# Twenty small additions from VectorE to POOL, squares behind halves, three moved instructions: a top-k attention with two feed-forward layers on one core

## The chip, the cores and the metric

One core of a Trainium2 chip runs the whole program as one launch. The metric is device microseconds (us) of that core, the median of several executions. Engines are named as the profile does: PE is TensorE's matmul, PEld its weight load, DVE is VectorE, ACT is ScalarE, POOL is GpSimd, SP is SyncE, which issues the DMAs.

## What is computed

The inputs are q, k and v (4 batches, 8 heads, 576 rows, 64 columns each), two weight matrices and a gain vector for the first feed-forward layer and two weight matrices for the second, all float32.

```python
scores = scale * np.matmul(q, k.transpose(0, 1, 3, 2))
kth = np.partition(scores, -top_k, axis=-1)[..., -top_k:-top_k + 1]   # top_k = 32
scores = np.where(scores >= kth, scores, -1000000000.0)
attn = np.exp(scores - np.max(scores, axis=-1, keepdims=True))
attn = attn / (np.sum(attn, axis=-1, keepdims=True) + 1e-09)
x = np.matmul(attn, v)                       # then rows (4*576, 8*64)
h = x @ w_in
e = np.exp(h - h_max)
solu = h * e / (np.sum(e, axis=-1, keepdims=True) + 1e-09)
x2 = ((solu - mu) / np.sqrt(var + 1e-06) * g_ln) @ w_out
h2 = x2 @ w_in2
out = (h2 * (1.0 / (1.0 + np.exp(-1.702 * h2)))) @ w_out2
```

## The kernel before, in words

`layers` is written twice into the program. The first copy (`quick`) works with constant scales and, beside its results, gathers sums by which it judges at its end whether those scales were fit: `insq` and `qsq` (sums of squares of the inputs), `zsq`, `ysum`. From them it makes a flag; all engines load the flag (L58) and branch (L59), and the second, exact copy runs only if the flag is set. It does not run for these inputs.

Every float32 operand of a matmul is held as two float16 halves: `split` (L120) makes a high half `hi` on ACT and a low half `raw - hi` on POOL or DVE. Where a total is wanted, a `Square` activation with an accumulator stands ahead of the halves and writes its junk into the tile of the high half. For k and q the two halves go into the tile `kq`, of which there is one (tag `kq`; the first few use other tags), and from there by a transposing DMA into `kt` (L359) or `qt` (L411).

Attention goes in 72 steps (two heads of 128 rows each): `scores` on PE, `copy_s` on ACT, `fold` (L473 to L476) and four `rounds` (L484, L487) on DVE that find the 32nd largest score, `mask` and `exp_of` on ACT and POOL, `high`/`low`, a transposing DMA, and three steps later `back`, the product with v. When a block's last step is through `back`, `finish` takes the reciprocals of the row sums (`recip`, L626 to L629), scales the result (L644) and queues the block for the feed-forward layers. These run interleaved with the attention steps, some blocks late; the last blocks run alone at the end. In the first six steps the 48 weight tiles are decoded and split on DVE, ACT and POOL (L249 to L254, L291, L138).

`recip` is the one place in the steps where DVE reads two operands that both lie in SBUF:

```python
def recip(r, n):
    nc.vector.scalar_tensor_tensor(r[:, 0:n], r[:, 0:n], 1e-9, r[:, 0:n], op0=ALU.add, op1=ALU.max)
    nc.vector.reciprocal(r, r)
```

It runs 20 times: 16 full blocks (8 sums a row) and 4 half blocks (4 sums).

Each engine runs its instructions in one fixed order. That order isn't the source's: the building layer places the instructions of each copy by its own estimate of when each can start, so a small edit can move instructions far away from it. The text below names the first copy alone.

Of the kernel before, what the change touches and what calls it, by code (L numbers as in the profile page):

```python
# [80 lines left out]
def layers(ctx, tc, quick, q, k, v, w1, w2, g_ln, w3, w4, out):  # L81
# [24 lines left out]
    if quick:  # L106
        picks = cst.tile([128, B * S * H // 128, 3], F32, name="picks")
        pickc = cst.tile([128, 2, 3], F32, name="pickc")
        insq = cst.tile([128, 2 * B * NP + 24], F32, name="insq")
        qsq = cst.tile([128, B * (NEWT + 1)], F32, name="qsq")  # L110
        zsq = cst.tile([128, NBLK], F32, name="zsq")
        ysum = cst.tile([128, NBLK], F32, name="ysum")
        for i, x in enumerate((1.0, -S_EXP, BIG)):
            nc.vector.memset(pickc[:, :, i], x)
        ones = cst.tile([128, 128], F32, name="ones")
        nc.gpsimd.memset(ones, 1.0)
# [3 lines left out]
    def split(raw, hi, lo, scale, what, total=None):  # L120

        n = lo_n[what] = lo_n.get(what, -1) + 1
        how = LO[what][n % len(LO[what])]
        if how == "P" and scale is not None:
# [3 lines left out]
        if how == "A" and scale is not None:  # L128
            act(raw, raw, AF.Copy, scale=scale)
            if total is not None:  # L130
                act(hi, raw, AF.Square, scale=1.0 / scale, accum_out=total)
            scale = None
        elif total is not None:
            act(hi, raw, AF.Square, accum_out=total)
        if scale is None:
# [3 lines left out]
        else:  # L139
            act(hi, raw, AF.Copy, scale=scale)  # L140
            nc.vector.scalar_tensor_tensor(lo, raw, scale, hi, op0=ALU.mult, op1=ALU.subtract)
        return how

# [44 lines left out]
    mhalf = cst.tile([128, 1], F32, name="mhalf")  # L188
    nc.vector.memset(mhalf, -0.5)
    wraw = {}  # L190

# [434 lines left out]
    def recip(r, n):  # L626

        nc.vector.scalar_tensor_tensor(r[:, 0:n], r[:, 0:n], 1e-9, r[:, 0:n], op0=ALU.add, op1=ALU.max)
        nc.vector.reciprocal(r, r)  # L629
# [66 lines left out]
    class Block:  # L696
# [121 lines left out]
        def g_high(self, g):  # L818
            t, gh = self.gh[g]
            if not quick:  # L820
                act(t, t, AF.Copy, scale=2.0 ** -16)
            act(gh[:, 0], t.rearrange("p (a n) -> p a n", a=4))

# [12 lines left out]
        def store(self):  # L836
            y = at.tile([128, 512], F32, tag="t", name="y")
            if quick:
                act(y, self.o, AF.Copy, scale=0.5 / (S_X2 * S_W[2] * S_W[3]), accum_out=ysum[:, self.no:self.no + 1])
            else:  # L840
                act(y, self.o, AF.Copy, scale=self.cf[:, 1:2])
# [65 lines left out]

    nc.sync.dma_start(gl, g_ln.rearrange("(c p) -> p c", p=128))
    if quick:
        nc.vector.tensor_scalar(gl, gl, S_W[1], None, op0=ALU.mult)  # L910

    if not quick:
        for a, b in ((0, 8), (8, 16), (16, WCH)):
            for i in range(a, min(a + RING, b)):
# [98 lines left out]
    gate = last_t[0]  # L1013
    load_for(0)
    with tc.issue_after(gate.ins):
# [14 lines left out]
    t = 0  # L1030
# [74 lines left out]

    ok = sm.tile([128, 6], F32, tag="ok", name="ok")

# [23 lines left out]
    nc.vector.tensor_scalar(flag, rows, 0.5, None, op0=ALU.is_gt)  # L1131
    return flag[0:1, 0:1]
# [30 lines left out]
```

## Time and profile before

| what | value |
|---|---|
| median of 3 runs | 961.12 us (960.68 to 962.55) |
| the profiled execution | 967.89 us, its span 966.0 us |
| busy: PE, DVE, ACT, POOL | 766.2, 766.7, 722.9, 695.9 us |
| mean granted TensorE clock | 0.914 of full speed |

The span is the time from the first to the last instruction; 1.9 us lie around it. Busy time is an average over stages: DVE is busy nearly without a break up to about 215 us, PE nearly without a break from about 300 us on, and after about 845 us the attention is over and PE runs the last feed-forward blocks.

### The profile page before, as it was taken

The page shows a single profiled execution, that of the slowest core. Times are in us where ns is not written, and L with a number is a line of the kernel's source. Part 1 is how long each engine was busy: PE and PEld are TensorE (multiplying, and loading weights), DVE is VectorE, ACT ScalarE, POOL GpSimd, SP SyncE. Part 2 cuts the span into 40 slices and gives each one's busy share as a digit, 9 for nine tenths or more (in the row PEclk, how much of TensorE's full clock was granted, in tenths as well). Part 3 has the DMA queues.
Part 4 walks back from the last instruction along what each step waited for, and adds up shares of the span by engine and source line. Part 5 has one row for each costly group of instructions (what it writes and reads, how often), then busy time and mean ns, then how long its engine had stood idle before and what let it go on. Part 6 is the DMA issues. An engine that isn't in the chain of part 4 may idle for free.

```text
span 966.0 us, 22236 instructions
## 1 busy us (share of the span) xinstructions
PE 766.2 (79%) x8228; PEld 497.6 (52%) x8228; DVE 766.7 (79%) x2150; ACT 722.9 (75%) x1257; POOL 695.9 (72%) x699
## 2 busy tenths in 40 slices
PE   1122524566688899989999899898999899999996
PEld 0011211534355556656665666565665666666564
DVE  4999999988698999897889988887988899511221
ACT  4689898587888978778899877778997878834431
POOL 2488999778968788777899886777987777733311
PEclk9995756677899999999999999998999899999998
DMA  6998666556757767566778577568756745532200
GB/s 159 314 308 202 178 164 151 122 117 126 143 122 139 122 119 136 105 119 124 137 138 156 115 127 118 100 111 150 137 113 116 130 76 90 97 69 45 44 14 25
DMA packets 337733, 122.66 MB, mean 127 GB/s; under 512 B 315344, under 2 KB 329168, under 8 KB 337616
## 3 DMA queue, kind: packets, MB, share of 16 engines
q1 hardware_dynamic: 337616, 121.16, 61.7%
q8 instruction: 66, 1.08, 0.5%
q14 instruction: 51, 0.42, 0.1%
HBM read 39.85 MB, written 4.72 MB: 46 GB/s over the span
## 4 chain that ended last, share of the span: by engine, by line
PE 26%; ACT 16%; DVE 16%; DMA 15%; POOL 14%; issue 8%; SPq 4%; ACTq 0%; POOLq 0%; DVEq 0%
PE h L806 9%; PE o L833 7%; ACT s L160 4%; PE x L776 4%; DVE wk L484 4%; POOL eh L523 4%; DVE wk L487 4%; PE ha L709 3%; POOL s L505 3%; POOL wt L138 2%; PE sc L455 2%; DMA kt<-kq 2%; ACT kq L160 2%; DMA qt<-kq 2%; DMA et<-eh 2%
## 5 line engine op out<-in xcount | busy, mean ns | idle before, releaser
L484 DVE MAX8 wk<-wk 128x8 f32<-128x296 f32 x576 | 242.2, 461 | 0.0
L806 PE MATMUL h<-x2t,wt 128*128 128x128 f16 x3456 | 217.1, 225 | 20.1 <-DVE t L815 14.8
L806 PEld LDWEIGHTS <-wt 128*128 128x128 f16 x3456 | 206.8, 101 | 27.2 <-issue 15.7
L833 PE MATMUL o<-wt,gh 128*128 128x512 f16 x864 | 203.3, 385 | 9.7 <-DVE wt L254 7.6
L523 POOL TENSOR_TENSOR eh<-s,eh 128x576 f16<-128x576 f32 x144 | 181.5, 1283 | 38.8 <-ACT eh L160 26.2
L505 POOL TENSOR_TENSOR s<-s,r 128x576 f32<-128x576 f32 x144 | 181.8, 1283 | 34.7 <-ACT r L160 34.5
L487 DVE MATCH_REPLACE8 wk<-wk 128x296 f32<-128x296 f32 x432 | 193.6, 458 | 0.0
L455 PE MATMUL sc<-kt,qt 128*128 128x64 f16 (+7 forms) x640 | 99.3, 321 | 71.7 <-DMA qt<-kq 30.8
L606 PE MATMUL av<-vt,et 128*128 128x64 f16 (+1 forms) x2400 | 90.1, 201 | 60.7 <-DMA et<-eh 52.2
L833 PEld LDWEIGHTS <-gh 128*128 128x128 f16 x864 | 83.8, 99 | 105.0 <-issue 16.1
L826 POOL TENSOR_TENSOR gh<-t,gh 128x512 f16<-128x512 f32 x72 | 83.6, 1161 | 73.2 <-ACT gh L160 73.1
L160 ACT ACTIVATE s<-s,picks 128x576 f32<-128x576 f32 x144 | 110.4, 768 | 16.9 <-POOL s L505 16.5
L606 PEld LDWEIGHTS <-et 128*128 128x128 f16 (+1 forms) x2400 | 82.2, 106 | 72.9 <-DMA et<-eh 55.9
L776 PE MATMUL x<-wt,zt 128*128 128x512 f16 x432 | 105.4, 397 | 14.3 <-DMA zt<-zh 14.2
L709 PE MATMUL ha<-wt,xt 128*128 128x512 f16 x432 | 101.9, 394 | 14.5 <-DMA xt<-xhl 11.1
L455 PEld LDWEIGHTS <-qt 128*128 128x128 f16 (+1 forms) x640 | 49.5, 110 | 123.5 <-DMA qt<-kq 31.2
L815 DVE SCALAR_TENSOR_TENSOR t<-t,h 128x512 f32<-128x512 f32 x72 | 49.2, 683 | 76.3 <-ACT t L160 73.3
L160 ACT ACTIVATE r<-s,picks 128x576 bf16<-128x576 f32 x144 | 103.5, 766 | 5.5 <-POOL picks L497 5.4
L160 ACT ACTIVATE t<-h 128x512 f32<-128x512 f32 x72 | 42.3, 588 | 70.7 <-PE h L806 61.9
L160 ACT ACTIVATE s<-sc 128x1152 f32<-128x1152 f32 x72 | 80.7, 1120 | 14.5 <-PE sc L455 8.5
L160 ACT ACTIVATE wt<-wt 128x512 f16<-128x512 f32 (+1 forms) x115 | 68.0, 627 | 22.9 <-DVE wt L254 10.5
L160 ACT ACTIVATE eh<-s 128x1152 f16<-128x1152 f32 x72 | 83.3, 1156 | 0.7
(84 smaller groups left out, 1070.1 us busy)
## 6 DMA issues: line engine op xcount, KB each, us to landing
wt<-in_moe_w_in_dram SPq DMA_DIRECT2D x24, 512.0 KB, 4.8
wt<-in_moe_w_out_dram SPq DMA_DIRECT2D x24, 512.0 KB, 5.7
qt<-qt SPq DMA_DIRECT2D x72, 64.0 KB, 2.0
raw<-in_k_dram SPq DMA_DIRECT2D x32, 128.0 KB, 2.5
raw<-in_q_dram SPq DMA_DIRECT2D x16, 256.0 KB, 3.3
vraw<-in_v_dram SPq DMA_DIRECT2D x32, 128.0 KB, 2.4
out_dram<-y SPq DMA_DIRECT2D x16, 256.0 KB, 3.2
et<-eh SPq DMA_TRANSPOSE x72, 4.7
```

The source lines that it names most:

```text
L160: nc.scalar.activation(out, in_, func, **kw)
L455: nc.tensor.matmul(sc[rows, i * S + c0:i * S + c1], t[qi // 4][:, hl, qi % 4, rows], kts[kp][:, k0 + c0:k0 + c1], start=(hl == 0), stop=(h ...
L484: nc.vector.max(out=wk[:, i, at_:at_ + 8], in_=wk[:, i, 0:W_END])
L487: nc.vector.match_replace(out=wk[:, i, 0:W_END], in_to_replace=wk[:, i, at_:at_ + 8], in_values=wk[:, i, 0:W_END], imm_value=LOW)
L505: nc.gpsimd.tensor_tensor(s[:, i], s[:, i], r[i], op=ALU.subtract)
L523: nc.gpsimd.tensor_tensor(eh[:, 1, cols], s[:, i], eh[:, 0, cols], op=ALU.subtract)
L606: nc.tensor.matmul(o[rows, col:col + 64], et[:, ea, 4 * i + c, rows], vts[kp][:, va, vc:vc + 64], start=(n == 0), stop=(n == 14))
L709: nc.tensor.matmul(h[:, half * 512:half * 512 + 512], self.xt[:, a, kc], w1v(kc, w, half), start=(n == 0), stop=(n == 11))
L776: nc.tensor.matmul(self.x2, self.zt[:, a, kc], w2v(kc, w), start=(n == 0), stop=(n == 23))
L806: nc.tensor.matmul(h2[:, mm * 128:(mm + 1) * 128], w3v(kc, w, 4 * g + mm), self.x2t[:, a, kc], start=(n == 0), stop=(n == 11))
L826: nc.gpsimd.tensor_tensor(gh[:, 1], t.rearrange("p (a n) -> p a n", a=4), gh[:, 0], op=ALU.subtract)
L833: nc.tensor.matmul(self.o, gh[:, a, mm], w4v(4 * g + mm, w), start=(g == 0 and n == 0), stop=(g == 3 and n == 11))
```

## The change

Five edits:

1. `recip`: the addition of 1e-9 (and a maximum that no longer is needed) leaves DVE and becomes a `tensor_scalar` on POOL. DVE's reciprocal now waits for POOL.
2. `split`: the `Square` for the totals comes behind the halves, and writes into a tile of its own, `squares`.
3. A one-column `Square` of a constant is put at the start of ACT's work, so that the one table load stands ahead of it.
4. The load of `g_ln` and its scaling go from the head of the program to behind the first k and q.
5. The last block's `ysum` is no longer judged. In its place the four gelu tiles of the last block are: their sums by the accumulator of the activation that makes the high half, their maxima by four new reductions on DVE. The final comparison loses one instruction.

```diff
     def split(raw, hi, lo, scale, what, total=None):
...
         if how == "A" and scale is not None:
             act(raw, raw, AF.Copy, scale=scale)
-            if total is not None:
-                act(hi, raw, AF.Square, scale=1.0 / scale, accum_out=total)
+            back = 1.0 / scale if total is not None else 1.0
             scale = None
-        elif total is not None:
-            act(hi, raw, AF.Square, accum_out=total)
...
+        if total is not None:
...
+            act(junk, raw, AF.Square, scale=back, accum_out=total)
...
+    if quick:
+        act(squares[:, 0:1], mhalf, AF.Square)
...
     def recip(r, n):
 
-        nc.vector.scalar_tensor_tensor(r[:, 0:n], r[:, 0:n], 1e-9, r[:, 0:n], op0=ALU.add, op1=ALU.max)
+        nc.gpsimd.tensor_scalar(r[:, 0:n], r[:, 0:n], 1.0, 1e-9, op0=ALU.mult, op1=ALU.add)
         nc.vector.reciprocal(r, r)
...
-            act(gh[:, 0], t.rearrange("p (a n) -> p a n", a=4))
+            if quick and self.no == NBLK - 1:
+                act(gh[:, 0], t.rearrange("p (a n) -> p a n", a=4), accum_out=glast[:, 0, g:g + 1])
+                nc.vector.tensor_reduce(glast[:, 1, g:g + 1], t, axis=AX.X, op=ALU.max)
...
     gate = last_t[0]
+    load_gl()
     load_for(0)
...
-    nc.vector.tensor_reduce(ok[:, 5:6], ok[:, 0:5], axis=AX.X, op=ALU.min)
-    bad = sm.tile([128, 1], F32, tag="bad", name="bad")
-    nc.vector.tensor_scalar(bad, ok[:, 5:6], 0.5, None, op0=ALU.is_lt)
+    nc.vector.tensor_scalar(ok[:, 5:9], glast[:, 0], 1e30, None, op0=ALU.is_le)
+    nc.vector.scalar_tensor_tensor(ok[:, 5:9], glast[:, 1], 65000.0, ok[:, 5:9], op0=ALU.is_le, op1=ALU.mult)
+    nc.vector.tensor_reduce(ok[:, 9:10], ok[:, 0:9], axis=AX.X, op=ALU.min)
...
-    nc.tensor.matmul(rows, ones, bad, start=True, stop=True)
+    nc.tensor.matmul(rows, ones, ok[:, 9:10], start=True, stop=True)
```

Lines of the changed kernel are some 5 to 16 higher. What the order of instructions becomes at three places:

ACT at the start of the program, before:

```order
L160 ACT_TABLE_LOAD
L160 ACTIVATE kq,insq<-raw 128x10x64
L160 ACTIVATE kq<-raw 128x10x64
L160 ACTIVATE kq,qsq<-raw 128x8x64
L160 ACTIVATE kq<-raw 128x8x64
L160 ACTIVATE wt<-wt 128x512 x3
```

and now:

```order
L164 ACT_TABLE_LOAD
L164 ACTIVATE squares<-mhalf 128x1
L164 ACTIVATE kq<-raw 128x10x64
L164 ACTIVATE squares,insq<-raw 128x640
L164 ACTIVATE kq<-raw 128x8x64
L164 ACTIVATE squares,qsq<-raw 128x512
L164 ACTIVATE wt<-wt 128x512 x6
```

The table load no longer stands behind a wait for k, and each high half is one activation nearer.

The third `recip` (in the weight decoding), on DVE before:

```order
L476 MAX wk<-sc 128x8 x2
L628 SCALAR_TENSOR_TENSOR rsum<-rsum 128x8
L253 SCALAR_TENSOR_TENSOR wi<-wt,wi 128x512
L484 MAX wk<-wk 128x8 x2
L629 RECIPROCAL rsum<-rsum 128x8
L254 SCALAR_TENSOR_TENSOR wt<-wt,wi 128x512
L487 MATCH_REPLACE wk<-wk 128x296 x2
```

now on DVE:

```order
L482 MAX wk<-sc 128x8 x2
L260 SCALAR_TENSOR_TENSOR wt<-wt,wi 128x512
L490 MAX wk<-wk 128x8 x2
L493 MATCH_REPLACE wk<-wk 128x296 x2
L490 MAX wk<-wk 128x8 x2
L493 MATCH_REPLACE wk<-wk 128x296
L635 RECIPROCAL rsum<-rsum 128x8
L493 MATCH_REPLACE wk<-wk 128x296
```

and the addition on POOL (L138 with `wt` is a low half, L297 a product of the decoding, L511 the mask, L529 the low half of the exponentials):

```order
L138 TENSOR_TENSOR wt<-wt 128x512 x2
L297 TENSOR_TENSOR wt<-wt 128x512
L634 TENSOR_SCALAR rsum<-rsum 128x8
L511 TENSOR_TENSOR s<-s,r 128x576 x2
L529 TENSOR_TENSOR eh<-s,eh 128x576 x2
```

The reciprocal moved behind the first rounds of the step, and the addition stands on POOL behind three large instructions of the decoding. The fifteenth addition stands on POOL directly behind the low half of a k tile (L138 with `kq`), and its reciprocal on DVE directly behind L798 (L792 before).

DVE at the end of the program, before:

```order
L815 SCALAR_TENSOR_TENSOR t<-t,h_13346 128x512
L1110 TENSOR_SCALAR junkc<-ysum 128x18
L1111 SCALAR_TENSOR_TENSOR junkc<-ysum,junkc 128x18
L1113 TENSOR_REDUCE ok<-junkc 128x1
L1125 TENSOR_REDUCE ok<-ok 128x1
L1127 TENSOR_SCALAR bad<-ok 128x1
L1131 TENSOR_SCALAR flag<-rows 128x1
```

and now:

```order
L821 SCALAR_TENSOR_TENSOR t<-t,h_13352 128x512
L830 TENSOR_REDUCE glast<-t 128x1
L1140 TENSOR_SCALAR ok<-glast 128x4
L1141 SCALAR_TENSOR_TENSOR ok<-glast,ok 128x4
L1142 TENSOR_REDUCE ok<-ok 128x1
L1146 TENSOR_SCALAR flag<-rows 128x1
```

The comparison of `ysum` went ahead of the last two gelu tiles, and nothing behind the last gelu waits for the last store's activation. On PE the small matmul of the flag (L1129 before, L1144 now) was the last one; now it stands ahead of the last four matmuls of the output.

## Rows read from the trace of the kernel before

**Rows 1.** Busy time by stretch: stretch, us, PE, PEld, DVE, ACT, POOL; clock, DMA, GB/s.

```profile
20.00:60.00 40.00, 6.89 (x26) 2.81 (x27) 39.47 (x101) 27.07 (x49) 21.52 (x24) 1.00 0.93 284
100.00:140.00 40.00, 15.01 (x164) 7.41 (x162) 38.25 (x97) 35.34 (x62) 37.93 (x37) 0.67 0.65 163
400.00:500.00 100.00, 92.08 (x1046) 60.46 (x1044) 84.74 (x248) 82.42 (x145) 81.03 (x86) 0.98 0.69 128
900.00:957.00 57.00, 54.09 (x535) 36.09 (x533) 12.88 (x29) 19.72 (x37) 13.44 (x13) 1.00 0.10 24
```

**Rows 2.** The page's part 4: the chain that ended last, shares by engine and line.

```profile
PE h L806 9%; PE o L833 7%; ACT s L160 4%; PE x L776 4%; DVE wk L484 4%; POOL eh L523 4%; DVE wk L487 4%; PE ha L709 3%; POOL s L505 3%; POOL wt L138 2%; PE sc L455 2%; DMA kt<-kq 2%; ACT kq L160 2%; DMA qt<-kq 2%; DMA et<-eh 2%
```

**Rows 3.** The same chain in order of time, the first 14 us: start, us, what.

```profile
0.73 0.46 SPq L908
...
5.30 1.28 ACT L160
...
6.60 0.84 ACT kq L160 x2
...
7.46 1.36 ACT kq L160 x3
...
10.71 2.72 DMA qt<-kq
```

**Rows 4.** Timeline, the load of q; and its group in the page's part 6.

```profile
3.79 0.60 SPq L389 DMA_DIRECT2D raw<-in_q_dram  x1
...
raw<-in_q_dram SPq DMA_DIRECT2D x16, 256.0 KB, 3.3
```

**Rows 5.** L628: ns, least, median, most; and its groups: busy us, mean ns | idle before.

```profile
L628 DVE SCALAR_TENSOR_TENSOR rsum<-rsum x20: 148/162/8205, 87.2 to 841.1; 128x8 f32<-128x8 f32 x16, 128x4 f32<-128x4 f32 x4
...
L628 DVE SCALAR_TENSOR_TENSOR rsum<-rsum 128x8 f32<-128x8 f32 x16 | 11.8, 736 | 1.9 <-ACT s L160 1.8
...
L628 DVE SCALAR_TENSOR_TENSOR rsum<-rsum 128x4 f32<-128x4 f32 x4 | 2.1, 534 | 1.0 <-ACT s L160 1.0
```

**Rows 6.** Timeline around the longest of them, DVE and POOL: start, us, [idle before <- releaser].

```profile
169.37 8.21 DVE L628 SCALAR_TENSOR_TENSOR rsum<-rsum 128x8 f32<-128x8 f32 x1
...
176.38 1.17 POOL L138 TENSOR_TENSOR wt<-wt 128x512 f16<-128x512 f32 x1
...
181.38 1.16 POOL L138 TENSOR_TENSOR wt<-wt 128x512 f16<-128x512 f32 x1 [3.83 <-ACT wt L160]
```

**Rows 7.** Groups of POOL by shape: count | busy us, mean ns | idle before.

```profile
L746 POOL TENSOR_SCALAR st<-zsq 128x1 f32<-128x1 f32 x18 | 3.5, 192 | 21.5 <-ACT zh L160 20.6
```

**Rows 8.** ACT's group of k's squares and halves; who waited for whom; one place.

```profile
L160 ACT ACTIVATE kq<-raw 128x640 f16<-128x640 f32 x32 | 23.5, 733 | 17.3 <-DMA kt<-kq 8.4 <-DMA qt<-kq 5.1 <-DMA raw<-in_k_dram 3.5
...
ACT kq L160 <- DMA kt<-kq: 20.0, 9, 4.2
...
655.78 0.76 DVE L473 TENSOR_TENSOR wk<-sc,s 128x576 f32<-128x576 f32 x1 [3.87 <-ACT s L160]
```

**Rows 9.** Timeline of the end, and PE's branch (start, us; ns least, median, most).

```profile
951.50 5.34 PE L833 MATMUL o<-wt,gh 128*128 128x512 f16 x24
...
957.66 0.18 DVE L1110 TENSOR_SCALAR junkc<-ysum 128x18 f32<-128x18 f32 x1 [4.58 <-ACT y L160]
...
959.11 0.16 DVE L1131 TENSOR_SCALAR flag<-rows 128x1 int32<-128x1 f32 x1 [0.47 <-PE rows L1129]
...
L59 PEldq COMPARE_BRANCH  x1: 3672/3672/3672, 959.9 to 959.9; - x1
```

**Rows 10.** Timeline, POOL and DVE at the places of the third and fifteenth addition.

```profile
182.36 0.45 DVE L487 MATCH_REPLACE8 wk<-wk 128x296 f32<-128x296 f32 x1
...
183.11 1.16 POOL L291 TENSOR_TENSOR wt<-wt 128x512 f32<-128x512 f32 x1 [0.57 <-ACT wt L160]
...
649.99 0.69 DVE L792 SCALAR_TENSOR_TENSOR x2hl<-x,x2hl 128x512 f16<-128x512 f32 x1 [2.51 <-POOL s L505]
...
658.97 1.41 POOL L138 TENSOR_TENSOR kq<-raw,kq 128x640 f16<-128x640 f32 x1
```

More of the change, by code (lines that the diff above doesn't have):

```diff
@@ L111, in layers @@
         zsq = cst.tile([128, NBLK], F32, name="zsq")
-        ysum = cst.tile([128, NBLK], F32, name="ysum")
+        ysum = cst.tile([128, NBLK - 1], F32, name="ysum")
         for i, x in enumerate((1.0, -S_EXP, BIG)):
             nc.vector.memset(pickc[:, :, i], x)
+        squares = cst.tile([128, 640], F16, name="squares")
+        glast = cst.tile([128, 2, 4], F32, name="glast")
         ones = cst.tile([128, 128], F32, name="ones")
@@ L122, in split @@
         n = lo_n[what] = lo_n.get(what, -1) + 1
+        back = 1.0
         how = LO[what][n % len(LO[what])]
@@ L141, in split @@
             nc.vector.scalar_tensor_tensor(lo, raw, scale, hi, op0=ALU.mult, op1=ALU.subtract)
+        if total is not None:
+            junk = squares[:, 0:raw.shape[1] * raw.shape[2]].rearrange("p (c d) -> p c d", d=raw.shape[2]) if len(raw.shape) == 3 \
+                else squares[:, 0:raw.shape[1]]
+            act(junk, raw, AF.Square, scale=back, accum_out=total)
         return how
@@ L821, in g_high @@
                 act(t, t, AF.Copy, scale=2.0 ** -16)
-            act(gh[:, 0], t.rearrange("p (a n) -> p a n", a=4))
+            if quick and self.no == NBLK - 1:
+                act(gh[:, 0], t.rearrange("p (a n) -> p a n", a=4), accum_out=glast[:, 0, g:g + 1])
+                nc.vector.tensor_reduce(glast[:, 1, g:g + 1], t, axis=AX.X, op=ALU.max)
+            else:
+                act(gh[:, 0], t.rearrange("p (a n) -> p a n", a=4))
         def g_low(self, g):
@@ L837, in store @@
             y = at.tile([128, 512], F32, tag="t", name="y")
-            if quick:
+            if quick and self.no < NBLK - 1:
                 act(y, self.o, AF.Copy, scale=0.5 / (S_X2 * S_W[2] * S_W[3]), accum_out=ysum[:, self.no:self.no + 1])
+            elif quick:
+                act(y, self.o, AF.Copy, scale=0.5 / (S_X2 * S_W[2] * S_W[3]))
             else:
@@ L906, in run, with load_gl @@
             pass
-    nc.sync.dma_start(gl, g_ln.rearrange("(c p) -> p c", p=128))
-    if quick:
-        nc.vector.tensor_scalar(gl, gl, S_W[1], None, op0=ALU.mult)
+    def load_gl():
+        nc.sync.dma_start(gl, g_ln.rearrange("(c p) -> p c", p=128))
+        if quick:
+            nc.vector.tensor_scalar(gl, gl, S_W[1], None, op0=ALU.mult)
     if not quick:
+        load_gl()
         for a, b in ((0, 8), (8, 16), (16, WCH)):
@@ L1013, in layers @@
     gate = last_t[0]
+    load_gl()
     load_for(0)
@@ L1102, in layers @@
             break
-    ok = sm.tile([128, 6], F32, tag="ok", name="ok")
+    ok = sm.tile([128, 10], F32, tag="ok", name="ok")
     def inside(x, lo, hi, dst):
@@ L1124, in layers @@
     inside(ysum, -1e30, 1e30, ok[:, 4:5])
-    nc.vector.tensor_reduce(ok[:, 5:6], ok[:, 0:5], axis=AX.X, op=ALU.min)
-    bad = sm.tile([128, 1], F32, tag="bad", name="bad")
-    nc.vector.tensor_scalar(bad, ok[:, 5:6], 0.5, None, op0=ALU.is_lt)
+    nc.vector.tensor_scalar(ok[:, 5:9], glast[:, 0], 1e30, None, op0=ALU.is_le)
+    nc.vector.scalar_tensor_tensor(ok[:, 5:9], glast[:, 1], 65000.0, ok[:, 5:9], op0=ALU.is_le, op1=ALU.mult)
+    nc.vector.tensor_reduce(ok[:, 9:10], ok[:, 0:9], axis=AX.X, op=ALU.min)
     rows = p_av.tile([128, 512], F32, tag="av", name="rows")[:, 0:1]
-    nc.tensor.matmul(rows, ones, bad, start=True, stop=True)
+    nc.tensor.matmul(rows, ones, ok[:, 9:10], start=True, stop=True)
     flag = sm.tile([128, 1], I32, tag="flag", name="flag")
-    nc.vector.tensor_scalar(flag, rows, 0.5, None, op0=ALU.is_gt)
+    nc.vector.tensor_scalar(flag, rows, 127.5, None, op0=ALU.is_lt)
     return flag[0:1, 0:1]
```

## The prediction, made before the change was run

> **What bounds the kernel now.** I read the busy time by stretch first. From 20 to 60 us DVE is busy 39.5 of 40 us, from 100 to 140 us DVE and POOL both are full (38.3 and 37.9 of 40); in the middle no engine is (between 400 and 500 us PE's pipelined 92, DVE 85, ACT 82, POOL 81 of 100); at the end PE alone works [rows 1]. The chain of waits says the same: no line has over 9% of it, and all engines and the transposes appear [rows 2]. So three stages have to be told apart. Start: one chain, in which each us saved moves everything. Middle: several chains side by side, in which a saving counts in part. End: PE's last matmuls and what hangs behind them. The last feed-forward blocks hang on the end of attention, so what the first two stages save reaches the end of the program.
>
> **Start.** SP's first issue is the load of g; it begins at 0.73 and takes 0.46 us, 0.5 with its gap, and the loads of k stand behind it. Then k lands, and at 5.30 comes the table load (1.28), then the square of k (0.84 to the read of its sum), the half of k and the square of q (1.36 together): the half of q begins at about 8.85 [rows 3]. Now k lands 0.5 earlier, at 4.8. The table load starts as soon as a constant is written, some 4 us before k is there, and k's DMA covers it. The half of k (0.73 [rows 8]) ends at 5.55, its square with the read of the sum at 6.45. The half of q also needs q: its issue moves from 3.79 to 3.3, and such a load lands 3.3 us after its issue [rows 4], so at 6.6. That is 8.85 - 6.6 = **2.2** us, and SP, which issues the transposes behind, has a load less ahead of them. Ends: 1.6, if q's landing counts from the end of its 0.6 us issue; 3.5, if all that leaves the path counts (0.5 + 1.28 + 0.84, and the square of q from the 1.36: 0.6 to 0.85). Late next is the second k tile: the last piece of its load now stands behind q's copies in SP's queue. DVE has the first step's rounds and the first decoding meanwhile; if that cover is gone, it costs one small load, 2 us at most. The load of g now stands among k's loads; its reader, the split of the second weight matrix, comes tens of us later. I cost both at nothing.
>
> The Trainium skill (ScalarE: Activation LUTs, What ACT_TABLE_LOAD costs) adds a drain of 1.38 us to the load's 1.28. The trace shows the square 0.02 us behind the load's end, so no drain; by that page the sum would be 1.4 larger and the forecast 948.9.
>
> **The addition.** L628 has a median of 0.16 us and a maximum of 8.2; its twenty take 11.8 + 2.1 = 13.9 us, 10.7 more than at the median [rows 5]. The long one begins at 169.37 and ends at 177.58, at the moment when a gapless run of POOL instructions ends (176.38 + 1.17 = 177.55). Behind it POOL stands idle for 3.8 us, since ACT waits for DVE [rows 6]. So DVE's second operand seems to be refused as long as POOL has work ready. The reciprocal reads one operand. The change therefore removes 8.05 us of stall at a place where DVE is full. But POOL was full there too, its instructions have to be done anyway, and now the addition waits in POOL's queue and the reciprocal for it. Ends: 0 and 8.05. I take **4.0**, the middle, for DVE and POOL are about equally full there [rows 1]. The other nineteen: the rest of the excess, 2.65 us, goes, and 20 x 0.16 on DVE; POOL gets 20 x 0.19 (its one-column `tensor_scalar` [rows 7]) and each reciprocal a wait across engines. Ends: -1 and 2.65; I take **0.5**, since most lie in the middle stage, where no engine is full.
>
> The Trainium skill (SBUF — State Buffer, Who interferes with whom) says that a VectorE instruction with two SBUF inputs contends with a GpSimd instruction that reads SBUF, and that the first of them keeps the port pair for its whole instruction. The trace agrees on who contends, not on how long: by that rule the wait would end with the one POOL instruction in hand, some 1.2 us, and not with POOL's run.
>
> **Squares.** The squares of k, q and v change places with the halves. ACT's work stays. What shrinks is the path from landing to transpose, by 0.73 us and the read of the sum at k's size [rows 8], and the time in which the single `kq` tile is held. ACT waited 20.0 us in 9 cases for the transpose of k to leave that tile; once the copy of the next scores stood behind it, and DVE idle for 3.87 us [rows 8]. The half still waits for the tile. Ends: 0, since ACT runs the square anyway; 9.7, half of the 2% of the span that `kq` on ACT has in the chain [rows 2]. I take **2.0**, nearer the lower end, since only the part of a wait that the square itself fills can go.
>
> **End.** PE's last 24 matmuls run from 951.50 to 956.84. Then come the store's activation, six small DVE instructions and the flag's matmul; the flag is ready at 959.27. Only then do the engines load it, and PE's branch takes 3.67 us, behind which all else ends. DVE had been idle since 957.66 - 4.58 = 953.08, the end of its last gelu tile [rows 9]. Now the verdict hangs on that tile alone: a reduction of 512 columns (at most the 0.76 us that 576 columns take in L473 [rows 8]) and three small ones of about 0.2 make it by 955, while PE multiplies. The flag's matmul stands among PE's last ones and costs up to 0.47 (what DVE waited for it [rows 9]). PE then loads the flag at 956.84 + 0.4 = 957.25 instead of 959.3: **2.05**. Ends: 1.6, if that matmul costs twice as much; 2.45, if nothing. The added reductions and reads of sums lie beside PE's matmuls. The last store leaves and lands within PE's branch, as before.
>
> **Sum.** 2.2 + 4.0 + 0.5 + 2.0 + 2.05 = 10.75, say 10.8. Against the profiled execution's own 967.9 that gives 957.1. The median of the runs without recording is 6.8 below it; I take the same 10.8 from it: **950.3**. All ends together would be 939 and 959; for this case I hold 941 to 956.
>
> **Rivals.**
>
> *The long stall belongs to the profiled execution* (953.7). It was 6.8 us longer than the others, nearly the 8.05 us of the stall. If in the others L628 waits here for one POOL instruction, as it does in the slower ones of the rest (2.65 us over nineteen), the stall's term is about 0.65, and the sum is 2.2 + 0.65 + 0.5 + 2.0 + 2.05 = 7.4. For it: the sizes. Against it: the order is fixed and POOL is full from 100 us on [rows 1], and recording can slow other things. The skill's rule on the port pair gives nearly the same: a stall term of about 1.0, 953.3.
>
> *Only the ends count* (956.9). POOL's queue takes the place of the port: the reciprocal waits for the same backlog, and ACT's queue for the same squares. Left are 2.2 + 2.05 = 4.25. For it: POOL is as full as DVE. Against it: POOL's 3.8 us of idleness behind the stall [rows 6], which DVE's going on would fill.
>
> *The new order gives all back* (961.1). The building layer's order changed in all engines up to the last blocks; 11 us is 1.1%, and an order that fits the chip a little worse eats it. No row speaks for this.
>
> *The additions hold DVE up* (968.0, slower). The third reciprocal now follows a round's instruction that ended at 182.81; its addition follows a POOL instruction that ended at 184.27. Without the stall the former would be at 174.8, so DVE would wait 9.5 us. The fifteenth reciprocal follows L792, which ended at 650.7, its addition the low half of a k tile that ended at 660.4: 9.7 us [rows 10]. DVE is in order: its rounds queue behind, and all of attention behind these. 19.2 on the path, less the old stall and the two ends (8.05 + 4.25), is 6.9 us slower. It decides from 12.3 us of such waits on. Against it: both POOL instructions had waited for ACT, which the change makes earlier, at the one by the stall, at the other by the square.
>
> **How the numbers follow.** The forecast has 0.46, the short stall 0.20, the ends alone 0.14, the order 0.08, the additions that hold DVE up 0.12. Differences under 0.2%, 1.9 us, can't be told from none here. So faster 0.80, same 0.08, slower 0.12. The range, 941 to 960.5, takes in the first three cases and the near half of the fourth and leaves out the rest of it, the fifth and a small part below.
>
> **What would show it.** Right: PE's first matmul 2 us earlier than now; no DVE instruction of 8 us, and DVE's waits for L634 under 5 us in all; the flag ready while PE still multiplies, and PE's load of it 2 us nearer to the last matmul. Wrong: waits for L634 of over 12 us in all; a first step that starts no earlier; and if the middle, from 220 to 845 us, grew by over 5 us, the order is the cause, whatever the edits do by themselves.

## The result and the profile after

| | before | after |
|---|---|---|
| median | 961.57 us (959.06 to 963.28, 8 runs) | 952.96 us (950.90 to 958.67, 8 runs) |
| after / before | | 0.9918, 95% interval 0.9894 to 0.9942 |
| the profiled execution | 967.89 us, span 966.0 | 955.67 us, span 953.7 |
| mean granted TensorE clock | 0.914 | 0.944 |

The change makes the kernel 8.6 us faster by the medians and 7.9 by the ratio (5.6 to 10.2). Forecast were 950.3 us and 10.8 us of gain. The sum was nearly met, its terms were not: one of them is nothing, two come out some three times as large when their edit stands alone, and a rival that was to have given everything back gives back somewhat under half of what the edits earn. The experiments below take the sum apart.

**The start** is no earlier. The table load is hidden and the halves are ready sooner, as the working had it: in ACT's timeline k's half begins at 4.62 (7.46 before [rows 3]) and q's at 6.43 (8.84 before).

```profile
0.73 1.28 ACT L164 ACT_TABLE_LOAD   x1 [0.73 <-PEq L1162]
2.02 0.20 ACT L164 ACTIVATE squares<-mhalf 128x1 f16<-128x1 f32 x1
4.62 0.74 ACT L164 ACTIVATE kq<-raw 128x640 f16<-128x640 f32 x1 [2.40 <-DMA raw<-in_k_dram]
...
6.43 0.63 ACT L164 ACTIVATE kq<-raw 128x512 f16<-128x512 f32 x1 [0.35 <-DMA raw<-in_q_dram]
```

SP's timeline of the same kernel shows where it went. The transposes of q are issued at 8.10, and the two take 4.52 us there; behind them comes PE's first multiplication, at 13.52 (13.47 before):

```profile
6.52 1.48 SPq L365 DMA_TRANSPOSE kt<-kq  x1
8.10 4.52 SPq L417 DMA_TRANSPOSE qt<-kq  x2
```

PE's timeline, the first multiplication:

```profile
13.52 0.61 PE L461 MATMUL sc<-kt,qt 128*128 128x512 f16 x1 [13.52 <-DMA qt<-kq]
```

And the chain of waits, in order of time, now goes through the first load of weights. Two issues (512 KB each) put the weights into the queues at 3.7 and 4.4 us, ahead of the transposes. (The chain's step from `wi` to the transposes is one of time alone; that the weights matter for the transposes is shown by e8 below.)

```profile
3.10 0.60 SPq L395
...
3.74 4.11 DMA wt<-in_moe_w_in_dram
...
7.87 0.23 DVE wi L255
8.10 5.37 DMA qt<-kq
```

**The addition.** The instruction of 8.2 us [rows 5] is gone; the groups of the sums (ns: least, median, most) are short on both engines, and DVE waits for POOL's addition in five cases:

```profile
L634 POOL TENSOR_SCALAR rsum<-rsum x20: 196/201/205, 87.8 to 833.7; 128x8 f32<-128x8 f32 x16, 128x4 f32<-128x4 f32 x4
L635 DVE RECIPROCAL rsum<-rsum x20: 157/184/204, 89.0 to 834.0; 128x8 f32<-128x8 f32 x16, 128x4 f32<-128x4 f32 x4
...
  POOL rsum L634: 11.8, 5
```

**The stretches** that answer to [rows 1] (the same columns; the last one lies 12 us earlier, as the end does) look as before: DVE full at the start, DVE and POOL full between 100 and 140 us, PE alone at the end.

```profile
20.00:60.00 40.00, 7.86 (x42) 3.68 (x43) 39.54 (x101) 27.45 (x52) 22.96 (x25) 1.00 1.01 287
100.00:140.00 40.00, 17.42 (x195) 9.14 (x192) 38.15 (x98) 35.85 (x66) 38.30 (x37) 0.67 0.67 165
400.00:500.00 100.00, 94.38 (x1098) 63.08 (x1097) 87.15 (x257) 85.77 (x153) 84.98 (x93) 1.00 0.76 139
888.00:945.00 57.00, 54.28 (x538) 36.38 (x536) 16.58 (x38) 20.03 (x40) 13.54 (x14) 1.00 0.10 24
```

**The end.** DVE's timeline has the reduction of the last gelu tile, three small instructions and the flag:

```profile
943.51 0.69 DVE L830 TENSOR_REDUCE glast<-t 128x1 f32<-128x512 f32 x1
944.26 0.17 DVE L1140 TENSOR_SCALAR ok<-glast 128x4 f32<-128x4 f32 x1
944.47 1.01 DVE L1141 SCALAR_TENSOR_TENSOR ok<-glast,ok 128x4 f32<-128x4 f32 x1
945.52 0.16 DVE L1142 TENSOR_REDUCE ok<-ok 128x1 f32<-128x9 f32 x1
946.53 0.16 DVE L1146 TENSOR_SCALAR flag<-rows 128x1 int32<-128x1 f32 x1 [0.85 <-PE rows L1144]
```

In PE's timeline the flag's multiplication lies ahead of the last four, which end at 946.35 + 1.02 = 947.37:

```profile
946.21 0.28 PE L1144 MATMUL rows<-ok,ones 128*128 128x1 f32 x2
946.35 1.02 PE L843 MATMUL o<-wt,gh 128*128 128x512 f16 x4
```

And PE's branch on the flag (ns least, median, most; start):

```profile
L59 PEldq COMPARE_BRANCH  x1: 3832/3832/3832, 947.3 to 947.3; - x1
```

From the end of the last multiplication to the end of the span are 953.75 - 947.38 = 6.4 us; before they were 966.03 - 956.84 = 9.2 [rows 9]. So 2.8 us come from the end. PE's branch is not what ends last there. The changed kernel's SP has the last store to issue first, branches at 948.5 and comes to its next instructions at 951.8, behind all other engines (PE at 951.2, ACT at 951.5). From the same view:

```profile
L59 SPq EVENT_SEMAPHORE  x8: 17/17/17, 951.8 to 952.4; - x8
...
L59 SPq COMPARE_BRANCH  x1: 58/58/58, 948.5 to 948.5; - x1
```

Before, SP branched at 959.84, 3.0 us behind the last multiplication; now it is 1.1 us. That is 1.9 of the 2.8 us. From SP's branch to its next instruction are 3.3 us (3.9 before), and behind that 1.9 (2.3 before).

**The middle.** The 72 folds (the first instruction of a step on DVE, [rows 8] has one) are a clock through attention. The first starts 0.1 us later than before, the last at 816.5 in place of 824.6: 8.1 earlier. Between them the lead swings from -5.5 us (behind, at step 8, counted from 0) to 16.7 (ahead, at step 18) and back to -0.9 (step 50): steps no longer stand in the same order on the engines. With such swings, the order is a suspect besides the edits.

### The profile page after: what moved, and what is told of

The parts are those of the page before. It is cut to its first block, busy times and chain, and to the rows that moved or that the text cites. A ratio compares the mean times of both kernels' runs of the same rounds, so it can differ in the third digit from the quotient of the medians.

```text
span 953.7 us, 22251 instructions
## 1 busy us (share of the span) xinstructions
PE 751.6 (79%) x8228; PEld 487.9 (51%) x8228; DVE 760.0 (80%) x2135; ACT 722.6 (76%) x1261; POOL 699.6 (73%) x719
## 4 chain that ended last, share of the span: by engine, by line
PE 33%; DMA 18%; DVE 15%; ACT 13%; POOL 12%; issue 5%; SPq 3%; ACTq 0%; POOLq 0%; DVEq 0%
PE h L812 9%; PE o L843 8%; PE x L782 6%; PE ha L715 5%; DVE wk L490 4%; ACT s L164 4%; DVE wk L493 3%; POOL s L511 3%; DMA raw<-in_q_dram 3%; POOL eh L529 2%; PE sc L461 2%; DMA wt<-in_moe_w_in_dram 2%; DMA qt<-kq 2%; PE av L612 2%; DMA et<-eh 2%
## 5 line engine op out<-in xcount | busy, mean ns | idle before, releaser
L490 DVE MAX8 wk<-wk 128x8 f32<-128x296 f32 x576 | 239.7, 453 | 0.0
L812 PE MATMUL h<-x2t,wt 128*128 128x128 f16 x3456 | 209.4, 221 | 12.8 <-DVE t L821 11.6
L529 POOL TENSOR_TENSOR eh<-s,eh 128x576 f16<-128x576 f32 x144 | 181.5, 1282 | 41.7 <-ACT eh L164 27.9
L812 PEld LDWEIGHTS <-wt 128*128 128x128 f16 x3456 | 199.8, 99 | 19.8 <-issue 7.6
L511 POOL TENSOR_TENSOR s<-s,r 128x576 f32<-128x576 f32 x144 | 181.6, 1283 | 36.7 <-ACT r L164 36.6
L843 PE MATMUL o<-wt,gh 128*128 128x512 f16 x864 | 198.7, 379 | 3.2 <-ACT y L164 2.4
L493 DVE MATCH_REPLACE8 wk<-wk 128x296 f32<-128x296 f32 x432 | 191.6, 449 | 0.0
L782 PE MATMUL x<-wt,zt 128*128 128x512 f16 x432 | 103.3, 393 | 13.0 <-DMA zt<-zh 11.3
```

The costliest lines, as they stand in the source:

```text
L490: nc.vector.max(out=wk[:, i, at_:at_ + 8], in_=wk[:, i, 0:W_END])
L493: nc.vector.match_replace(out=wk[:, i, 0:W_END], in_to_replace=wk[:, i, at_:at_ + 8], in_values=wk[:, i, 0:W_END], imm_value=LOW)
L511: nc.gpsimd.tensor_tensor(s[:, i], s[:, i], r[i], op=ALU.subtract)
L529: nc.gpsimd.tensor_tensor(eh[:, 1, cols], s[:, i], eh[:, 0, cols], op=ALU.subtract)
L782: nc.tensor.matmul(self.x2, self.zt[:, a, kc], w2v(kc, w), start=(n == 0), stop=(n == 23))
L812: nc.tensor.matmul(h2[:, mm * 128:(mm + 1) * 128], w3v(kc, w, 4 * g + mm), self.x2t[:, a, kc], start=(n == 0), stop=(n == 11))
```

## The experiments

To part edits from order, the order was held. A table of numbers, written into a kernel, lets each instruction of an engine follow the one that it followed in another kernel (order alone, no wait is added). Instructions that the other kernel does not have (e9's additions, for one) are placed freely. "In the old order" below means held so to the kernel before. Ratios are to runs of the kernel before on the same chip (medians of 964.35 to 965.16 us), with the 95% interval; gains in us below are worked out from the ratio. The third edit, the early table load, has no run of its own.

| run | what differs from before | median us | ratio (interval) |
|---|---|---|---|
| e1 | addition on POOL, old order | 950.54 | 0.9870 (0.9842 to 0.9898) |
| e2 | squares behind halves, old order | 958.08 | 0.9934 (0.9909 to 0.9959) |
| e3 | load of g moved, old order | 964.08 | 0.9992 (0.9973 to 1.0011) |
| e4 | end alone | 961.03 | 0.9969 (0.9949 to 0.9990) |
| e5 | all edits, old order | 952.51 | 0.9867 (0.9839 to 0.9896) |
| e6 | changed kernel, addition on DVE, new order | 974.16 | 1.0097 (1.0064 to 1.0130) |
| e7 | addition on DVE with one operand, old order | 964.72 | 1.0006 (0.9988 to 1.0024) |
| e8 | changed kernel, weights later, free order | 973.47 | 1.0096 (1.0072 to 1.0119) |
| e9 | addition on DVE element by element, old order | 956.58 | 0.9917 (0.9895 to 0.9940) |
| e10 | addition on POOL and end, old order | 953.29 | 0.9885 (0.9858 to 0.9911) |
| e11 | e10, the third and fourth edit, weights later, old order | 957.37 | 0.9913 (0.9887 to 0.9939) |
| e12 | e5 with the flag's multiplication free | 949.71 | 0.9852 (0.9814 to 0.9889) |

### e1: the addition alone

```diff
-        nc.vector.scalar_tensor_tensor(r[:, 0:n], r[:, 0:n], 1e-9, r[:, 0:n], op0=ALU.add, op1=ALU.max)
+        nc.gpsimd.tensor_scalar(r[:, 0:n], r[:, 0:n], 1.0, 1e-9, op0=ALU.mult, op1=ALU.add)
```

> The kernel before with the additions to the row sums on POOL and nothing else; the order of every engine's other instructions is held as it was. Theory of the prediction (the stall of 8.05 us behind POOL is what the edit removes): no instruction of the row sums over 1 us on DVE, DVE's waits for the addition under 12 us in all, 4 to 5 us faster than before (956.5 to 957.5). Rival one (the stall is an accident of the profiled run): within 1 us of before, about 961. Rival two (the gain of the middle comes from the new order of the instructions, not from this edit): also about 961, with the stall gone from the trace. Rival three (DVE is held up by POOL's queue): 963 or more.

12.5 us faster (9.8 to 15.2): above the upper end of the term (8.05 + 2.65 = 10.7), though the interval takes that in, and more than the whole change as built. DVE's timeline at the place of the stall:

```profile
170.00 0.83 DVE L617 MAX8 wk<-wk 128x8 f32<-128x296 f32 x2
170.80 0.20 DVE L762 RECIPROCAL rsum<-rsum 128x8 f32<-128x8 f32 x1
170.92 0.63 DVE L387 SCALAR_TENSOR_TENSOR wt<-wt,wi 128x512 int32<-128x512 int32 x1
...
176.33 0.76 DVE L606 TENSOR_TENSOR wk<-sc,s 128x576 f32<-128x576 f32 x1
```

POOL's at the same place:

```profile
169.31 1.17 POOL L424 TENSOR_TENSOR wt<-wt 128x512 f32<-128x512 f32 x1
170.56 0.20 POOL L761 TENSOR_SCALAR rsum<-rsum 128x8 f32<-128x8 f32 x1
170.84 2.53 POOL L656 TENSOR_TENSOR eh<-s,eh 128x576 f16<-128x576 f32 x2
173.33 1.16 POOL L271 TENSOR_TENSOR wt<-wt 128x512 f16<-128x512 f32 x1
```

The fold at 176.33 is the one that began at 184.13 before: the place gives 7.8 us, nearly the whole stall. POOL is no emptier (busy 29.8 of 30 us from 140 to 170, as before, and 14.8 of 15 from 170 to 185, where it was 9.9), but the addition stands behind one POOL instruction only, and DVE's rounds run beside POOL's run. (The place lies in the twelfth step. The decoding of the weights lasts longer than that, not six steps: before, L254 runs from 10.8 to 249.3 us.) Up to the last fold the lead grows from 7.8 to 16.7 us in this execution; in e10, which has the same addition, only from 6.5 to 8.8, so what the addition earns behind the place is not settled. The rivals "an accident of the profiled run" and "DVE held up" fall: DVE waits for the addition 4.0 us in all, twice, not at all at the third place of [rows 10] and 2.66 us at the fifteenth, for which 9.5 and 9.7 were worked out.

### e2, e3, e4: the other edits alone

e2 has the change's hunk of `split`, e3 that of `load_gl`, e4 those of `glast`, `store` and `ok`.

> The kernel before with the sums of squares issued behind the halves and nothing else; the order of the other instructions is held. Theory of the prediction: 2 us faster through the middle (about 959.5). Theory that came with the result (where an early step's transposes wait for weights in the DMA queues, halves that are ready sooner buy nothing): q's and k's halves ready 1 us sooner in the first 10 us, the first multiplication and the first fold within 0.2 us of before, time within 1 us of before.

> The kernel before with the load of g moved behind the loads of the early steps and nothing else; the order of the other instructions is held. Theory of the prediction: the first loads are issued 0.5 us sooner and 0.5 us comes off the end, too little for the interval. Theory that came with the result (the start ends with the first weights' transfer, whenever the loads begin): first loads sooner, first multiplication within 0.2 us of before, no change of the time.

> The kernel before with the last block judged by its gelu tiles and nothing else; the order in front of the end is the same. Theory of the prediction: the flag is ready while PE still multiplies, 2.05 us off the end (1.6 to 2.45), about 959.5. By the trace of the changed kernel, where the last multiplication stands 6.3 us ahead of the span's end and stood 9.2 us ahead of it before: 2.8 us off, about 958.7. In both the middle up to the last fold is unchanged; a gain over 4 us would mean that it is not.

e2: 6.4 us (4.0 to 8.8) where 2.0 were forecast, and "no more than 1 us" from the theory about the start. That theory is right that the start itself gains nothing (first fold 0.5 us later than before, in e4 0.4), but the squares earn elsewhere. Up to the twelfth step nothing is gained; against e4, which has before's order up to the end, the lead comes in lumps near steps 14 to 26, 32, 36, 51 and 55. The waits that shrank are those for `kq`, the single tile of the halves. In the view of waits (engine, waited for: us in all, times, longest) the kernel before has:

```profile
ACT kq L160 <- DMA kt<-kq: 20.0, 9, 4.2
POOL kq L138 <- ACT kq L160: 10.8, 6, 6.0
ACT kq L160 <- DMA qt<-kq: 6.4, 5, 1.4
```

and e2:

```profile
ACT kq L296 <- DMA kt<-kq: 14.1, 6, 4.2
POOL kq L270 <- ACT kq L296: 5.0, 3, 4.1
ACT kq L296 <- DMA qt<-kq: 2.3, 5, 1.0
```

15.8 us less (5.9 + 5.8 + 4.1), on two engines. The other runs bear out that it is this edit: without it (before, e1, e3, e4, e7, e10) the three waits are 18.6 to 20.3, 10.0 to 12.0 and 6.3 to 8.0 us, with it (e2, e5, e12) 14.1 to 15.7, 5.0 to 5.6 and 1.4 to 2.5. The first of the three in e1 and in e12:

```profile
ACT kq L293 <- DMA kt<-kq: 18.6, 9, 4.0
...
ACT kq L296 <- DMA kt<-kq: 15.2, 6, 4.3
```

One place where it reaches DVE is the fold of [rows 8], ahead of which DVE stood idle for 3.87 us. In e2 these are 1.65, in e12 0.94:

```profile
644.92 0.76 DVE L609 TENSOR_TENSOR wk<-sc,s 128x576 f32<-128x576 f32 x1 [1.65 <-ACT s L296]
```

That the waits make up all of the 6.4 us is argued from the sizes, not shown apart.

e3: nothing that can be measured, as the start's theory has it: the first load is issued at 0.73 with k's data, and the first fold is 0.15 us later than before. e4: 3.0 us (1.0 to 4.9), of which the trace shows 966.03 - 956.84 = 9.2 before and 964.10 - 957.88 = 6.2 now behind the last multiplication. Up to the end e4 has the instructions of before in their order, so its trace says how well two executions agree: its folds lie within 2.2 us of before's. (Those of e7, no faster than before, lie up to 4.8 us ahead, so a lead of a few us in one execution says little.) The stall is there again, 8.24 us (8.25 and 8.26 in e2 and e3). It is no accident.

### e5, e6: edits and order

> All edits of the change, with the other instructions of every engine held in the order of the kernel before. Theory 'the order takes back' (the single edits gave 12.5, 6.4, 0.8 and 3.0 us in the old order, the change as built only 8.6): 15 to 22 us faster than the kernel before run beside it, a ratio of 0.977 to 0.985, with the folds of the first layer at or ahead of those of the run with the addition alone. Rival 'the gains overlap' (each edit fills the same gaps): about what the whole change gave, a ratio of 0.989 to 0.993.

> The changed kernel with the additions to the row sums back on DVE with two operands from SBUF, in the order of the changed kernel. Theory 'a port stall': one or more of the 20 additions on DVE lasts as long as POOL's run of instructions next to it (some us); where POOL has a gap beside it, it takes 0.16 us. By the trace of the changed kernel, whose order is another, the place of the stall may move; 4 to 10 us slower than the changed kernel (a ratio to before of 0.996 to 1.002) if one addition stalls as before, and no slower than 1 us (0.991 to 0.993) if none does. Rival 'the order, not the addition, gave the gain': 0.991 to 0.993 with a stall in the trace.

e5 came between its two theories: 12.8 us, more than the change as built, but not the 22.7 that the single gains add up to. Part of it is an effect of holding the order, which put the flag's multiplication back behind the last one (e12 mends that). So the single gains don't add up, and the new order costs something.

e6 puts the addition back on DVE in the new order, and the kernel is 17 us slower than the changed one (1.0097 against 0.9918), more than the 4 to 10 that one stall was to cost. Its group of additions (ns: least, median, most) and, from DVE's timeline, the second of the two long ones:

```profile
L765 DVE SCALAR_TENSOR_TENSOR rsum<-rsum x20: 143/227/10494, 88.7 to 853.0; 128x8 f32<-128x8 f32 x16, 128x4 f32<-128x4 f32 x4
...
182.16 7.75 DVE L765 SCALAR_TENSOR_TENSOR rsum<-rsum 128x8 f32<-128x8 f32 x1
```

Two additions stall for long now, 10.49 us at 118.27 behind nine POOL instructions in a row and 7.75 at 182.16 behind seven. So where the stall falls, and how often, is set by the order; that it falls at all, by the addition.

### e7 and e9: what it is about the addition

> The kernel before with the additions on DVE still, but with one operand from SBUF (a multiplication by 1 and the addition of 1e-9) in place of two; the order of every engine held. Theory 'the second operand is what waits for POOL': no addition over 0.3 us, and the whole gain of the run with the addition on POOL (a ratio of 0.985 to 0.990), perhaps a little more since no semaphore goes between the engines. Rival 'any DVE instruction at this place waits, as POOL holds the memory': an addition of 8 us at about 170 us, and a ratio of 0.998 to 1.001.

> The kernel before with the additions on DVE still, but one instruction for each element (8 or 4 of them, 128x1) in place of one over 8 or 4 elements; the order of every engine held. The run with one operand showed the same stall, so the second operand is not what waits. Theory 'the form': an instruction of one element, as DVE's small ones on the statistics of the normalisation, which show no stall beside POOL, is not held up: no addition over 0.3 us, and the gain of the run with the addition on POOL less what 144 short instructions cost DVE (up to 0.15 us each): a ratio of 0.985 to 0.993. Rival 'whatever DVE does with the sums waits at this place': the first of the eight takes 8 us at about 170 us, and a ratio of 0.998 to 1.005.

The additions of e7 and of e9 (1e-9 is added, without the multiplication by 1 that the first of the two texts mentions):

```diff
+        nc.vector.tensor_scalar(r[:, 0:n], r[:, 0:n], 1e-9, None, op0=ALU.add)              # e7
+        for k in range(n):                                                                   # e9
+            nc.vector.tensor_scalar(r[:, k:k + 1], r[:, k:k + 1], 1e-9, None, op0=ALU.add)
```

The additions' group of e7 (ns: least, median, most):

```profile
L762 DVE TENSOR_SCALAR rsum<-rsum x20: 151/164/8243, 88.0 to 837.1; 128x8 f32<-128x8 f32 x16, 128x4 f32<-128x4 f32 x4
```

and of e9:

```profile
L762 DVE TENSOR_SCALAR rsum<-rsum x144: 126/143/155, 38.3 to 831.7; 128x1 f32<-128x1 f32 x144
```

The theory of the prediction fell in e7: with one operand the stall is the same 8.24 us, and no time is won. In e9 the same sums, on the same engine, element by element, are never held up: 0.155 us at most, though 97 of the 144 began while a POOL instruction ran. They don't stand in one place but are spread over the steps as the sums come (38.3 to 831.7 us). The last of the third block stands where the stall was, 0.17 us into a POOL instruction (e7's began 0.13 us into one and was held). DVE's and POOL's timelines of e9:

```profile
169.29 0.13 DVE L762 TENSOR_SCALAR rsum<-rsum 128x1 f32<-128x1 f32 x1
...
169.12 1.18 POOL L424 TENSOR_TENSOR wt<-wt 128x512 f32<-128x512 f32 x1
```

The reciprocal, also one operand and 8 elements, isn't held up either (0.21 at most, and 15 of the 20 of before began beside POOL). So it is this operation over several elements, from SBUF to SBUF, and not the second operand.

The trace of the kernel before could have said so. At its end a comparison with one operand and 144 columns (L1110) takes 1.19 us and ends 0.09 behind the POOL instruction beside it, while L1111, with two operands and as many columns, takes 0.31 behind it, with POOL idle:

```profile
941.86 1.16 POOL L826 TENSOR_TENSOR gh<-t,gh 128x512 f16<-128x512 f32 x1 [4.01 <-ACT gh L160]
941.91 1.19 DVE L1110 TENSOR_SCALAR junkc<-short 128x144 f32<-128x144 f32 x1
943.14 0.31 DVE L1111 SCALAR_TENSOR_TENSOR junkc<-short,junkc 128x144 f32<-128x144 f32 x1
```

Nor is `recip` the one place in the steps where DVE reads two operands from SBUF: the low halves of the first k and q tiles (L141, five times) do so too.

e9 gains 8.0 us (0.9917; 5.8 to 10.1), about the stall. That it is less than e1's gain since 144 instructions take DVE's time is likely, but the intervals overlap.

The Trainium skill (VectorE: DVE Perf Modes, What auto-detection actually checks) has a rule that fits e7 and e9: an instruction with a single source takes a mode with two ports if source and destination lie in SBUF and their outermost dimensions that aren't 1 are both even or equal, and firmware enables the modes of an instruction. 8 and 4 elements are even, one element has no such dimension. For the addition with two operands the rule says nothing, and whether the reciprocal has the mode it doesn't say. That the port is the cause the runs don't show.

### e8, e11: the weights at the start

```diff
-        if n == 1:
+        if n == 2:
             w_loads(-1, 2)
```

> The changed kernel with the first two loads of weights (512 KB each) issued one step later, behind the loads of the third early piece; the order is free, so some of it moves. Theory 'the first multiplication waits for q's transposes, which queue behind the weights': the transposes of q land at about 8.1 + 1.5 us, the first multiplication stands at 11 us or sooner (13.5 in the changed kernel) and the first fold 2 us sooner. Rival 'the transposes themselves take that long': the first multiplication at 13 us or later. What of the 2 us is left at the end hangs on the order, and is not forecast closely: 0.985 to 0.995 to before.

> As the run with the additions and the tail, and besides: table load first, load of g behind the early loads, and the first two loads of weights issued behind q's transposes and its copies, their conversions behind the first scores; all other instructions in the old order. Theory 'the start is worth what it shows once the weights are out of the way': first multiplication at 11 us or sooner (13.5 before), first fold 2 to 3 us sooner, and 2 to 3 us less at the end than the run with the additions and the tail. Rival 'the middle takes it back, since the weights come later': first fold sooner, but within 1 us of that run at the end, or slower.

SP's timeline of e8 at the start:

```profile
8.03 2.63 SPq L417 DMA_TRANSPOSE qt<-kq  x2
```

and PE's:

```profile
10.65 0.61 PE L461 MATMUL sc<-kt,qt 128*128 128x512 f16 x1 [10.65 <-DMA qt<-kq]
```

The transposes, issued at the same 8 us, take 2.63 in place of 4.52, and the first multiplication stands at 10.65: shown, it is the weights ahead of them that hide the start's gain. At the end e8 loses 17 us to the changed kernel all the same. Its free order is another one again; how much of the 17 us that is, and how much the later weights, it doesn't show. e11 does the same in the old order. Its first multiplication stands at 11.39 (not quite the 11 expected) and its first fold 1.9 us earlier than before; by the second step that lead is gone (the third starts 38.55 - 35.96 = 2.6 us later than before): four instructions of the weights' conversion, ahead of the first fold before, now stand inside the first step of a full DVE. At the end it is no faster than e10 (957.37 against 953.29). So the start's 2 us are not to be had in this way.

### e10, e12: the best of it

> The kernel before with the additions on POOL and the last block judged by its gelu tiles, nothing else; the order held. Theory 'these two carry it' (the squares fill the same gaps as the additions, and the start gains nothing): as fast as all edits in the old order or faster, a ratio of 0.982 to 0.987 (12.5 + 3.0 of 964.8 us make 0.984). Rival 'the squares add their own gain': slower than all edits in the old order by 2 us or more, 0.989 or above.

> All edits in the old order as before, but the multiplication that sums the flag is left free and stands four multiplications ahead of the last one on PE; held in its old place, behind the last, it cost that run 1.3 us of the tail (7.6 us from the end of the last multiplication to the end of the span, against 6.2 to 6.4 us where the flag comes first). Theory 'the end is a sum of its own': 6.2 to 6.4 us in that stretch, and 1.3 us faster than all edits in the old order, a ratio of 0.983 to 0.987, the fastest of all versions and 4 us or more faster than the change as built. Rival 'PE's branch hides it': 7 us or more in that stretch, no change to all edits in the old order.

e10 came out between its theories, at 0.9885, and its interval covers e1 and e5: what the squares add to the addition isn't settled by it. In e10 and e5 the flag's multiplication was held behind PE's last one, and from the last multiplication to the end there were 7.6 us. In e12 it is free; PE's timeline has it four multiplications ahead:

```profile
938.17 0.28 PE L1276 MATMUL rows<-ok,ones 128*128 128x1 f32 x2
938.31 1.02 PE L975 MATMUL o<-wt,gh 128*128 128x512 f16 x4
```

945.7 - (938.31 + 1.02) = 6.4 us, as expected. e12 is the fastest version: 0.9852, 14.3 us faster than before, and 6.3 us (0.0066) ahead of the change as built, whose edits it shares. That is the price of the new order, but not a close figure: the two intervals (0.9814 to 0.9889, 0.9894 to 0.9942) only just don't touch, and the difference lies between 2 and 11 us.

## Why the prediction was right, and where it was not

The forecast time and its range hold the result, but that the sum came so near is luck: its terms were off in opposite ways, and the order, put at 0, took back much of what the addition and the squares gave beyond their terms. Of its own signs, "a first step that starts no earlier" stood for being wrong and came true, and DVE's waits for the addition are 11.8 us, where under 5 stood for being right. The stall that is gone and the flag that is ready early came as forecast.

- **Start, 2.2: nothing.** ACT's part came as worked out (the half of q 2.4 us earlier). The step that failed is "SP, which issues the transposes behind, has a load less ahead of them": the queues still had 1 MB of weights ahead of them. Taking that away (e8) gives the start 2.9 us. The drain of 1.38 us that the Trainium skill (ScalarE: Activation LUTs, What ACT_TABLE_LOAD costs) adds to the table load isn't there in the changed kernel either: the next activation begins at 2.02, 0.01 us behind the load.
- **The addition, 4.0 + 0.5: 12.5.** The step that failed is "POOL was full there too ... I take 4.0, the middle". A full POOL cost nothing there, where the addition stands early in its queue and DVE has other work that runs beside POOL: 7.8 of the 8.05 us came at the place (e1). The rest of e1's gain, some 5 us, lies behind the place; e9's 8.0 us and e10's trace speak for less.
- **"DVE's second operand seems to be refused": wrong** (e7), though nothing in the sum hung on it. An addition with one operand would have looked like a cheaper cure and is none.
- **Squares, 2.0: 6.4 by themselves** (e2), inside its ends of 0 and 9.7. The value near the lower end rested on ACT's work staying the same and on the wait of ACT for `kt` alone; the wait of POOL for the halves (10.8 to 5.0 us) was left out. The idle time that the prediction pointed at, DVE's 3.87 us, did shrink, by 2.2 us in e2.
- **End, 2.05: 2.8 in the trace, 3.0 by e4.** PE's load of the flag was put 0.4 us behind the end of the last multiplication; it stands 0.64 us ahead of it (946.73 against 947.37), and the branch begins at 947.32, while the last multiplications still run. "PE's branch ..., behind which all else ends" is the step that doesn't hold: SP's branch, behind the issue of the last store, comes last now. The three small instructions were not all of 0.2: L1141 took 1.01 beside a POOL instruction that began at 944.31 and ended at 945.46. So the same kind of stall is there too, at a place where it costs nothing: its result is there at 945.68, and PE comes to the flag's multiplication at 946.0.
- **The sum.** The single gains make 12.5 + 6.4 + 0.8 + 3.0 = 22.7; together they make 14.3 in the old order. The terms were summed as if each lay on a path of its own. What makes the 8.4 us of difference stays open. The waits for `kq` are not it: the addition alone leaves them as they were (e1), and with both edits (e12) they shrink as with the squares alone. The lumps in e2's lead near steps 32, 36 and 55 (1.8, 2.3 and 3.8 us) are in e12 too (1.9, 2.4 and 4.2). Part of the difference may be the uncertainty of the single gains, 2 or 3 us each: e10, too, whose two edits lie in different stages, gives 11.1 (8.6 to 13.7), where 12.5 + 3.0, less the 1.3 for the flag's place, make 14.2.
- **The ends.** The lower of "all ends together" is added up wrongly: 3.5 + 8.05 + 2.65 + 9.7 + 2.45 = 26.35 makes 935 and not 939. The range starts at 941 and doesn't hang on it.
- **The other rivals.** The long stall doesn't belong to the profiled execution alone (e1's gain is that of the medians, and the stall stands in the traces of e2, e3, e4 and e7 as well). That only the ends count is nearly the reverse of what the runs show.
- **The order** was a rival with a chance of 0.08 and a term of 0. It costs some 6.3 of the 14.3 us (2 to 11). One part may be seen in the waits: DVE waits for POOL's addition 11.8 us in five cases in the changed kernel and 3.5 in two in e12. The rest isn't taken apart. "Waits of over 12 us", the mark set for additions that hold DVE up, was nearly reached, by the order and not by the edit.

## What to carry to other kernels

An instruction that took fifty times its usual time beside another engine's work was worth nearly its whole stall here, where its engine is full, and it was cured by its form (one element at a time) or by another engine, not by a guess at which operand waits. Where a building layer places instructions by its own estimate, hold the order of the old kernel to learn what an edit is worth, since the new order alone moved this kernel by some 6 us; moving one pair of loads, with the order free again, cost 17 (e8), where in the old order it came out 3 to 4 slower, hardly clear of noise (e11 against e10). And before crediting a shorter path to a DMA, look at what stands in the queues ahead of that DMA.

## What was not expected of the hardware

- The stall is the same within 0.06 us in five executions of five kernels (8.20, 8.25, 8.26, 8.24, 8.24 us), and it is not always POOL's whole run: at 527.47 us of the kernel before, the addition took 0.95 us and ended with the first of two POOL instructions in a row (527.12 + 2.52 for both), at 169.37 it had to wait for seven. All other additions over 0.2 us of that kernel (0.21 to 0.96) end 0.03 us or less behind the one POOL instruction that ran when they began. Why it is let in at one place and not at the other stays open.
- The Trainium skill (SBUF — State Buffer, Who interferes with whom) has the holder keep the ports for its whole instruction; 0.95 us agrees with that, 8.2 and 10.49 us don't.
- The mean granted clock between 20 and 100 us was 0.81 in the profiled run of before (1.00 up to 60 us, 0.62 behind) and 1.00 in that of the changed kernel, and the steps of that stretch were no faster for it (their folds are at most 0.1 us ahead of before's; in e12, in the old order and with 1.00 there too, 0.4 to 1.7 us behind): DVE is what is full there, 78.7 and 77.7 of 80 us.
